# Column sums for a linear-attention denominator: two DMA transposes and a VectorE reduction in place of ten one-column matmuls

## The chip, the cores and the metric

The kernel runs on one core of one Trainium2 chip. Times are device microseconds (us) of that core. A run's time (about 210 us) is some 2 us longer than the span that its profile shows (about 208 us, first to last instruction).

Engines: PE is TensorE's matmul row, PEld its weight loads, DVE is VectorE, ACT is ScalarE, POOL is GpSimd, SP is SyncE, which here issues the DMAs.

## The reference, cut to what matters

```python
xn = _layernorm(x)                                     # 2048 tokens x 640
q, k, v = split(xn @ wqkv)                             # 32 heads of 20
pq, pk = phi(q), phi(k)
kv  = einsum("bhsd,bhse->bhde", pk, v)
z   = einsum("bhsd->bhd", pk)                          # the token sums
num = einsum("bhqd,bhde->bhqe", pq, kv)
den = einsum("bhqd,bhd->bhq", pq, z)[..., None] + 1e-6
out = x + (num / den) @ wo + gelu(xn @ w1 + b1) @ w2 + b2
```

z is one number for each of the 640 columns of phi(k), summed over 2048 tokens. The change concerns only how z gets from "one partial sum per partition" to "one number per column, on the partition where it is needed".

## The kernel before

The kernel plans its instructions by hand. The order in which an engine's instructions are written is the order in which they run in these traces (in the changed kernel's, DVE starts the five ZB products at 105.51 us and the first q unit's operation only at 106.73, though that unit's exp ended at 105.87). It works in stages: layer norm and the gelu branch's first matmuls; the K stage (phi(k) into `PK`); the GT stage (160 matmuls of `PK` and the normalised tokens); the q units (five per chunk of 512 tokens, each five matmuls, an exp on ACT and two DVE operations); the KVT and M steps between the chunks; the denominator (den); and the output matmuls.

During the GT stage DVE adds the sixteen token tiles of `PK` into `zsum` (128 partitions x 640, float) and splits the sum into a bf16 hi and lo part. Then ten matmuls against a column of ones sum each part over the partitions. Column j + 5m of the sums lands on partition m, column j of z.

```python
def z_step():
    b = zbank
    Pl.ins("tensor", [(lambda e, j=j, i=i: e.matmul(bank(b, j, j + 1), zhl[:, i, j:D:DT], onesb[:],
                                                    start=(i == 0), stop=(i == 1)))
                      for j in range(DT) for i in range(2)],
           reads=[r_zhl, r_small], writes=[B_[b]])
    Pl.ins(v, lambda e: e.tensor_copy(z_sb[:], bank(b, 0, DT)), reads=[B_[b]], writes=[r_z])
    for j in range(DT):
        Pl.ins(v, lambda e, j=j: e.tensor_scalar(ZB[:, j, :], bmask[:], z_sb[:, j:j + 1], None, ALU.mult), ...)

def token_sum():
    # ... cut: zsum = sum of the 16 tiles PK[:, t, :], 15 additions
    Pl.ins(v, lambda e: e.tensor_copy(zhl[:, 0, :], zsum), reads=[r_zsum], writes=[r_zhl])
    Pl.ins(v, lambda e: e.tensor_tensor(out=zhl[:, 1, :], in0=zsum, in1=zhl[:, 0, :], op=ALU.subtract), ...)

token_sum()
for f in range(DT):
    b = take(2)
    zbank = (b + 3) % 8
    if f == DT - 1:
        z_step()                      # between GT blocks 4 and 5 in PE's order
    # ... cut: 32 GT matmuls of block f, then ACT copies the two banks out

def phi(src, b, nb, dst, ...):        # one unit: ACT exp, then two operations on DVE
    # exp into one of three buffers ek; min and add in place; max(src, 0) + ek into dst, which frees the bank

q_chunk(0); kvt_step(); q_chunk(1); q_chunk(2); m_step(); q_chunk(3)
# ... cut: den_step() reads ZB; then the output matmuls
```

PSUM's eight banks are handed out in a ring by `take`. The M step takes five pairs of banks, and its fourth pair is the one that the last two q units of chunk 2 used: it must wait until DVE is done with them.

## Time and profile before

| | before |
|---|---|
| time, median of 3 runs | 210.2 us (210.06 to 210.44) |
| span in the profile | 207.9 us |
| PE busy | 203.1 us, 98% |
| DVE busy | 108.1 us, 52% |
| ten ones matmuls on the chain of waits | 0.36 us |
| DVE idle between ZB and the first q unit | 4.56 us |

From the page of the kernel before: busy time by engine, the granted PE clock in forty slices (tenths of full speed), the DMA share in the same slices, and the chain of work that ended last.

```profile
PE 203.1 (98%) x1592; PEld 140.4 (68%) x1598; DVE 108.1 (52%) x226; ACT 74.3 (36%) x141; POOL 21.1 (10%) x59
PEclk9999999999999999999999999999999999999999
DMA  5999779997000000000000000681111111001001
PE 91%; DVE 4%; DMA 3%; issue 1%; ACTq 0%; DVEq 0%
```

PE is the limit: it is busy for 98% of the span, at full clock (1.00 on average over the span), and is 91% of the chain. The DMA engines are idle through the middle of the kernel (share 0.00 from 54 to 124 us).

The chain of waits of the kernel before, pieces in order of time (start, duration, what), around the place that is changed.

```profile
81.80 17.39 PE ps L511 x128
99.18 0.36 PE ps L485 x10
99.54 4.37 PE ps L511 x32
...
122.72 0.70 DVE PQ L463
123.43 0.14 issue
123.56 1.29 PE ps L548 x32
```

The ten ones matmuls (L485) sit in PE's stream between four blocks of GT matmuls and the fifth. The part cut here follows DVE from 115.22 on: its operations for the q units come one unit after another every 1.08 us, which is PE's own pace. The last three lines are the one place downstream where PE follows DVE closely: DVE ends the last q unit of chunk 2 at 123.42, and the M step's fourth group (L548) begins at 123.56.

The timeline of the kernel before (start, duration, engine, line, operation, out<-in; in brackets the idle time before it and who ended it).

```profile
96.63 0.49 DVE L500 CAST Msb<-Msb 128x640 bf16<-128x640 f32 x1
97.16 0.83 DVE L501 TENSOR_TENSOR Msb<-Msb 128x640 bf16<-128x640 f32 x1
99.58 0.17 DVE L489 COPY z_sb<-ps 128x5 f32<-128x5 f32 x1 [1.60 <-PE ps L485]
99.78 1.32 DVE L491 TENSOR_SCALAR ZB<-bmask,z_sb 128x32 bf16<-128x32 bf16 x5
105.03 0.60 ACT L460 ACTIVATE ek<-ps 128x512 bf16<-128x512 f32 x1 [0.38 <-PE ps L523]
105.66 0.29 DVE L461 TENSOR_SCALAR ek<-ek 128x512 bf16<-128x512 bf16 x1 [4.56 <-ACT ek L460]
```

The first two lines make hi and lo. DVE is done with z at 101.1 and is idle until the first q unit: it starts that unit 0.03 us after the exp ends (105.03 + 0.60 to 105.66).

The twelve DMA transposes that the kernel already makes near its start, from the view of their source line.

```profile
L444 SPq DMA_TRANSPOSE xnT<-xn_tm x12: 1200/1277/2067, 15.1 to 31.0; - x12
DMA to landing us min/median/max: 2.6/3.0/4.7
```

Each takes SP's queue about 1.28 us, and its data land 2.6 to 4.7 us after issue starts.

### The profile page before, as it was taken

The page shows a single profiled execution, that of the slowest core. Times are in us where ns is not written, and L with a number is a line of the kernel's source. Part 1 is how long each engine was busy: PE and PEld are TensorE (multiplying, and loading weights), DVE is VectorE, ACT ScalarE, POOL GpSimd, SP SyncE. Part 2 cuts the span into 40 slices and gives each one's busy share as a digit, 9 for nine tenths or more (in the row PEclk, how much of TensorE's full clock was granted, in tenths as well). Part 3 has the DMA queues.
Part 4 walks back from the last instruction along what each step waited for, and adds up shares of the span by engine and source line. Part 5 has one row for each costly group of instructions (what it writes and reads, how often), then busy time and mean ns, then how long its engine had stood idle before and what let it go on. Part 6 is the DMA issues. An engine that isn't in the chain of part 4 may idle for free.

```text
span 207.9 us, 3963 instructions
## 1 busy us (share of the span) xinstructions
PE 203.1 (98%) x1592; PEld 140.4 (68%) x1598; DVE 108.1 (52%) x226; ACT 74.3 (36%) x141; POOL 21.1 (10%) x59
## 2 busy tenths in 40 slices
PE   7899999999999999999999999999999999999995
PEld 2799886444457777777756565577777777777775
DVE  4689960000008888998268865474863422523322
ACT  2689887666676445111153577100000000000000
POOL 3245567000041000000000000000000000000000
PEclk9999999999999999999999999999999999999999
DMA  5999779997000000000000000681111111001001
GB/s 167 343 358 110 119 123 152 372 324 249 3 0 0 0 3 0 0 3 0 0 3 2 0 3 0 202 309 47 71 59 57 63 39 54 32 32 35 32 34 62
DMA packets 22698, 17.98 MB, mean 86 GB/s; under 512 B 9240, under 2 KB 22680, under 8 KB 22680
## 3 DMA queue, kind: packets, MB, share of 16 engines
q1 hardware_dynamic: 22000, 17.24, 29.5%
q10 hardware_dynamic: 680, 0.49, 0.9%
q8 instruction: 12, 0.20, 0.4%
q14 instruction: 6, 0.05, 0.1%
HBM read 12.62 MB, written 2.62 MB: 73 GB/s over the span
## 4 chain that ended last, share of the span: by engine, by line
PE 91%; DVE 4%; DMA 3%; issue 1%; ACTq 0%; DVEq 0%
PE ps L612 33%; PE ps L352 25%; PE ps L511 10%; PE ps L473 10%; PE ps L523 7%; DVE PQ L463 3%; DMA W<-in_B_w_dram 3%; PE ps L648 2%; DVE ek L461 1%; PE ps L532 1%; PE ps L548 1%; PE ps L558 1%; PE ps L382 1%; PE ps L336 0%; ACTq L233 0%
## 5 line engine op out<-in xcount | busy, mean ns | idle before, releaser
L352 PE MATMUL ps<-xnT,W 128*128 128x128 bf16 (+2 forms) x432 | 51.8, 281 | 0.2
L612 PE MATMUL ps<-W,HG 128*128 128x320 bf16 x360 | 51.0, 299 | 0.0
L352 PEld LDWEIGHTS ps<-xnT,W 128*128 128x128 bf16 x435 | 35.5, 98 | 15.6
L612 PEld LDWEIGHTS ps<-W,HG 128*128 128x128 bf16 x360 | 35.1, 98 | 14.2 <-issue 0.4
L356 ACT ACTIVATE HG<-ps,b1c 128x128 bf16<-128x128 f32 (+2 forms) x87 | 40.0, 492 | 12.5 <-PE ps L352 10.3
L461 DVE TENSOR_SCALAR ek<-ek 128x512 bf16<-128x512 bf16 (+1 forms) x36 | 11.1, 308 | 41.7 <-ACT ek L460 40.5
L460 ACT ACTIVATE ek<-ps 128x512 bf16<-128x512 f32 (+1 forms) x36 | 23.2, 644 | 19.8 <-PE ps L523 10.1
L631 DVE TENSOR_TENSOR out_sb<-ps,xnT 128x640 bf16<-128x640 f32 x15 | 12.4, 825 | 33.5 <-PE ps L612 33.3
L612 PE MATMUL ps<-Msb,PQ 128*128 128x320 bf16 x150 | 22.3, 299 | 0.0
L511 PE MATMUL ps<-xPK,xn_tm 128*128 128x320 bf16 x160 | 22.1, 299 | 0.0
L473 PE MATMUL ps<-Wqkv,xnT 128*128 128x320 bf16 x160 | 21.9, 299 | 0.0
L523 PE MATMUL ps<-xnT,Wqkv 128*128 128x512 bf16 x97 | 21.4, 379 | 0.3 <-issue 0.2
L473 PEld LDWEIGHTS ps<-Wqkv,xnT 128*128 128x128 bf16 x160 | 15.6, 98 | 6.3
L511 PEld LDWEIGHTS ps<-xPK,xn_tm 128*128 128x128 bf16 x160 | 15.6, 98 | 6.0
L612 PEld LDWEIGHTS ps<-Msb,PQ 128*128 128x128 bf16 x150 | 14.6, 98 | 5.7
L523 PEld LDWEIGHTS ps<-xnT,Wqkv 128*128 128x128 bf16 x100 | 11.6, 118 | 9.6 <-ACT Msb L553 0.2
L463 DVE SCALAR_TENSOR_TENSOR PQ<-ps,ek 128x512 bf16<-128x512 f32 x20 | 13.8, 692 | 2.1
L308 DVE BATCH_NORM_STATS2 stats<-xPK 128x6 f32<-128x320 bf16 x32 | 13.6, 466 | 2.5 <-DMA xPK<-in_A_x_dram 2.4
L463 DVE SCALAR_TENSOR_TENSOR xPK<-ps,ek 128x640 bf16<-128x640 f32 x16 | 13.2, 825 | 1.7
L498 DVE TENSOR_TENSOR Msb<-Msb,xPK 128x640 f32<-128x640 f32 x14 | 11.6, 826 | 0.5
L515 ACT ACTIVATE W<-ps 128x640 bf16<-128x640 f32 x5 | 3.5, 703 | 18.6 <-PE ps L511 18.6
L318 POOL TENSOR_TENSOR rstd<-aggr,mhalf 128x1 f32<-128x1 f32 x16 | 9.1, 568 | 8.9 <-DVE aggr L316 8.9
(62 smaller groups left out, 90.6 us busy)
## 6 DMA issues: line engine op xcount, KB each, us to landing
xnT<-in_A_x_dram SPq DMA_DIRECT2D x4, 640.0 KB, 6.6
Wqkv<-in_A_wqkv_dram SPq DMA_DIRECT2D x3, 800.0 KB, 6.4
out_dram<-out_sb SPq DMA_DIRECT2D x15, 160.0 KB, 1.8
W<-in_B_w_dram SPq DMA_DIRECT2D x1, 1920.0 KB, 15.6
W<-in_B_w_dram SPq DMA_DIRECT2D x3, 480.0 KB, 6.8
xPK<-in_A_x_dram SPq DMA_DIRECT2D x2, 640.0 KB, 9.4
Wo<-in_A_wo_dram SPq DMA_DIRECT2D x1, 800.0 KB, 10.9
xPK<-in_A_x_dram SPq DMA_DIRECT2D x4, 160.0 KB, 4.2
```

What stands on the lines that cost most here:

```text
L308: Pl.ins(v, lambda e: e.bn_stats(stats[:, s, 6 * h:6 * h + 6], x_in[:, t, h * HW:(h + 1) * HW]), reads=[r_x[t]], writes=[r_stats[s][h]])
L352: Pl.ins("tensor", [(lambda e, k=k: e.matmul(bank(b, 0, w), W1[:, k, jb * P:(jb + 1) * P], xnT[:, k, tok], start=(k == 0), stop=(k == DT - ...
L356: Pl.ins("scalar", lambda e: e.activation(HG[:, jb, tok], bank(b, 0, w), ACT.Gelu_apprx_tanh, bias=b1c[:, jb:jb + 1]), reads=[B_[b], r_b1c ...
L460: Pl.ins("scalar", lambda e: e.activation(e2, src, ACT.Exp), reads=br, writes=[r_ek[s]])
L461: Pl.ins(v, lambda e: e.tensor_scalar(et, et, 1.0, 1e-6, ALU.min, ALU.add), reads=[r_ek[s]], writes=[r_ek[s]])
L463: Pl.ins(v, lambda e: e.scalar_tensor_tensor(out=d2, in0=src, scalar=0.0, in1=e2, op0=ALU.max, op1=ALU.add), reads=br + [r_ek[s]], writes= ...
L473: fns.append(lambda e, k=k, h=h, b=b, t=t: e.matmul(bank(b + h, 0, HW), xnT[:, k, t * P:(t + 1) * P], Wqkv[:, k, D + h * HW:D + (h + 1) * ...
L498: Pl.ins(v, lambda e, t=t: e.tensor_tensor(out=zsum, in0=zsum, in1=PK[:, t, :], op=ALU.add), reads=[r_PK[t], r_zsum], writes=[r_zsum])
L511: Pl.ins("tensor", [(lambda e, t=t, h=h, b=b, f=f: e.matmul(bank(b + h, 0, HW), xn_tm[:, t, f * P:(f + 1) * P], PK[:, t, h * HW:(h + 1) * ...
L523: Pl.ins("tensor", [(lambda e, k=k, j=j, b=b: e.matmul(bank(b), Wqkv[:, k, j:D:DT], xnT[:, k, cc], start=(k == 0), stop=(k == DT - 1))) fo ...
L612: return lambda e: e.matmul(bank(b + h, 0, HW), l, r[:, h * HW:(h + 1) * HW], start=(i == 0), stop=(i == JT + DT - 1))
L631: Pl.ins(v, lambda e: e.tensor_tensor(out=halves(out_sb[:, s, :]), in0=pair(b), in1=halves(x_res[:, t, :]), op=ALU.add), reads=B_[b:b + 2] ...
```

## The change

Its intent: take the ten matmuls off the engine that is the limit, and let engines that are idle there (DMA with its share of 0.00, DVE with its 4.56 us before the first q unit) do the sum over partitions. A DMA transpose turns "640 columns on 128 partitions" into "128 values in a row for each column", and DVE adds along the row. So that column j + 5m lands on partition m, hi and lo are now written in the order (j, m), which makes DVE read `zsum` with a stride of five floats. In DVE's order the wait for the DMA now lies before the q units.

```diff
         def z_step():
-            b = zbank
-            Pl.ins("tensor", [(lambda e, j=j, i=i: e.matmul(bank(b, j, j + 1), zhl[:, i, j:D:DT], onesb[:],
-                                                            start=(i == 0), stop=(i == 1)))
-                              for j in range(DT) for i in range(2)],
-                   reads=[r_zhl, r_small], writes=[B_[b]])
-            Pl.ins(v, lambda e: e.tensor_copy(z_sb[:], bank(b, 0, DT)), reads=[B_[b]], writes=[r_z])
+            zT = out_sb[:].rearrange("p a (j q) -> p a j q", j=DT)
+            for i in range(2):
+                Pl.ins("sync", lambda e, i=i: e.dma_start_transpose(zT[:, i], zhl[:, i, :]),
+                       reads=[r_zhl], writes=[r_out[i]], dma=True)
+            Pl.ins(v, lambda e: e.tensor_reduce(out=z_sb[:], in_=zT.rearrange("p a j q -> p j a q"),
+                                                axis=mybir.AxisListType.XY, op=ALU.add),
+                   reads=r_out, writes=[r_z])
             # ... unchanged: ZB from bmask and z_sb
         def token_sum():
             # ... unchanged: zsum
-            Pl.ins(v, lambda e: e.tensor_copy(zhl[:, 0, :], zsum), reads=[r_zsum], writes=[r_zhl])
-            Pl.ins(v, lambda e: e.tensor_tensor(out=zhl[:, 1, :], in0=zsum, in1=zhl[:, 0, :], op=ALU.subtract),
+            zs = zsum.rearrange("p (m j) -> p j m", j=DT)
+            zp = zhl.rearrange("p a (j m) -> p a j m", j=DT)
+            Pl.ins(v, lambda e: e.tensor_copy(zp[:, 0], zs), reads=[r_zsum], writes=[r_zhl])
+            Pl.ins(v, lambda e: e.tensor_tensor(out=zp[:, 1], in0=zs, in1=zp[:, 0], op=ALU.subtract),
                    reads=[r_zsum, r_zhl], writes=[r_zhl])

         token_sum()
+        z_step()
         for f in range(DT):
             b = take(2)
-            zbank = (b + 3) % 8
-            if f == DT - 1:
-                z_step()
```

## The prediction

> **What bounds the kernel now.** TensorE: busy 203.1 of 207.9 us (page, busy time), full granted clock in every slice; the chain of work that ended last is 91% PE, and PE's waits sum to about 2 us, nearly all at the start. VectorE is at 52%; the DMA engines idle from about 52 to 125 us. So only what changes PE's stream, or makes PE wait, moves the time.
>
> **The stage touched** (timeline, 80 to 130 us). PE runs the 160 GT matmuls (PK and xn) from 81.63. DVE meanwhile adds the token sums (83.74 to 98.0). The ten 128x1 ones matmuls sit before the last GT block, at 99.02, and take 0.36 us of the chain. DVE waits 1.60 us for them, copies z (0.17 us), builds ZB (5 x 0.234 us, done at 101.1), then idles 4.56 us until the first q unit's exp, at 105.66. ZB's reader, the den matmuls, comes only at 133.57.
>
> **What the change does.**
> - Removes ten weight loads and ten matmuls from PE: about -0.4 us, all critical. GT then ends near 103.5, not 103.91, and the first q unit wants DVE near 105.25.
> - Removes the 0.17 us copy from PSUM.
> - The sums are read with a stride of five floats. The cast (0.493 us) should fall to its neighbour's 0.826; the subtract stays at 0.83. hi and lo are ready near 98.35.
> - Adds two DMA transposes on the SP queue. The twelve in this trace take 1.28 us of issue each and land 2.6 us (least; median 3.0) after issue starts. Issues near 98.4 and 99.7; the second lands near 102.4. [...]
> - Adds a reduction of 128x1280 bf16 on DVE. [...] From the instructions here that read PSUM (512 elements 0.69 us, 640 elements 0.825, so 1.06 ns each plus 0.15) I estimate 1.5 us: 102.4 to 104.0. ZB follows until about 105.4.
>
> **How much is critical.** DVE, in order, now waits about 4 us for DMA, in a gap that was idle anyway. It starts the q units about 0.1 to 0.3 us late. In that stage PE makes a unit every 1.08 us and DVE can do one every 1.00 when behind; DVE next holds PE at the banks of the M step (123.41 against 123.55). Counting DVE's work without gaps (15 units and 1.95 us of KVT masks) gives an estimated 0.8 us of slack. So the late start is absorbed and the PE saving stays: about -0.4 us.
>
> **Prediction.** 209.8 us, 80% range 209.3 to 210.7. Faster by over 2%: 0.01; within 2%: 0.97; slower by over 2%: 0.02.
>
> **What would show the steps right.** GT one run of 160 matmuls ending 0.4 us earlier; transposes issued near 98.4 and 99.7, the second landing near 102.4; DVE waiting 3.5 to 4.5 us for DMA; a reduction near 1.5 us; the first q unit's DVE operation at most 0.5 us behind its exp; no new PE wait in the M step.
>
> **What would make it wrong.** Transposes landing over 1 us later, [...] or a reduction over 2.5 us: DVE then starts the q units over 1 us late, the slack is used up, and PE waits for PSUM banks in the q stage or M step, up to 1 us for each further us, as PE has no room to make it up. Slower by 2% (4 us) needs a delay of about 5 us.

210.2 us less the 0.4 us of the ones matmuls is 209.8 us, and the late start of 0.1 to 0.3 us stays below the slack of 0.8 us and adds nothing.

## The result, and the profile after

The changed kernel took 209.86 us (median of 6 runs, 209.46 to 210.53) against 210.2 us for the kernel before in the same rounds. The ratio is 0.9987, with a 95% interval of 0.9968 to 1.0006. Ratios here are the mean time of one kernel's fast runs over that of the other's of the same rounds, so they are not quite the ratio of the medians. In a second set of rounds (e_after_again below) the ratio was 0.9982, interval 0.9970 to 0.9994. So the change is within 2%. The medians put it 0.3 to 0.5 us ahead; the first interval still includes no change, the second does not.

From the page of the changed kernel: busy time by engine, and the chain of work that ended last.

```profile
PE 203.1 (98%) x1582; PEld 140.3 (67%) x1588; DVE 109.7 (53%) x226; ACT 74.3 (36%) x141; POOL 21.1 (10%) x59
PE 94%; DMA 3%; DVE 1%; issue 0%; ACTq 0%; DVEq 0%
```

PE has ten matmuls fewer (1592 to 1582). Its busy total hides the gain, because PE worked longer before the GT stage: the first load of weights on the chain of waits took 5.86 us in place of 5.20, and the GT stage began 0.63 us later. Both lie before the place that was changed.

The chain of waits of the changed kernel in the same place.

```profile
82.42 21.73 PE ps L512 x160
...
122.97 0.70 DVE PQ L463
123.67 0.14 issue
123.81 1.29 PE ps L549 x31
```

The GT stage is one run of 160 matmuls, 21.73 us, where it took 17.39 + 0.36 + 4.37 = 22.12 us before: 0.39 us less. The meeting point at the M step has the same 0.14 us as before, so nothing was given back there.

The timeline of the changed kernel for the same instructions.

```profile
97.26 1.31 DVE L503 CAST Msb<-Msb 128x640 bf16<-128x640 f32 x1
98.61 1.31 DVE L504 TENSOR_TENSOR Msb<-Msb 128x640 bf16<-128x640 f32 x1
99.95 2.53 SPq L486 DMA_TRANSPOSE out_sb<-Msb  x2
103.99 1.49 DVE L488 TENSOR_REDUCE z_sb<-out_sb 128x5 f32<-128x1280 bf16 x1 [4.07 <-DMA out_sb<-Msb]
105.27 0.60 ACT L460 ACTIVATE ek<-ps 128x512 bf16<-128x512 f32 x1 [0.38 <-PE ps L524]
105.51 1.31 DVE L492 TENSOR_SCALAR ZB<-bmask,z_sb 128x32 bf16<-128x32 bf16 x5
106.73 0.29 DVE L461 TENSOR_SCALAR ek<-ek 128x512 bf16<-128x512 bf16 x1
...
122.57 0.29 DVE L461 TENSOR_SCALAR ek<-ek 128x512 bf16<-128x512 bf16 x1
122.97 0.69 DVE L463 SCALAR_TENSOR_TENSOR PQ<-ps,ek 128x512 bf16<-128x512 f32 x1
```

Cast and subtract take 1.31 us each (before 0.49 and 0.83). DVE waits 4.07 us for the transposes. The reduction takes 1.49 us. The first exp ends at 105.87 and DVE takes it up only at 106.73, so DVE is 0.86 us behind (before: 0.03). By the last unit of chunk 2 it has caught up: that exp (not shown) ends at 122.54 and DVE starts at 122.57.

The execution starts 0.6 us later in this trace than in the one before, so from here on I use a stretch without the start: **from the start of the first GT matmul to the start of the last output addition**. Before: 81.63 to 205.65, 124.02 us. After: 82.26 to 205.90, 123.64 us. The change is worth -0.38 us. The end points in the two timelines, first before and then after (of each line only the start counts):

```profile
81.63 4.65 PE L511 MATMUL ps<-xPK,xn_tm 128*128 128x320 bf16 x33
205.65 0.29 DVE L651 TENSOR_TENSOR out_sb<-ps,xnT 128x128 bf16<-128x128 f32 x1 [0.59 <-PE ps L648]
82.26 3.97 PE L512 MATMUL ps<-xPK,xn_tm 128*128 128x320 bf16 x28
205.90 0.29 DVE L652 TENSOR_TENSOR out_sb<-ps,xnT 128x128 bf16<-128x128 f32 x1 [0.59 <-PE ps L649]
```

The expectations below were written with end points that differ by up to 0.2 us from these, so read their differences and not their absolute figures.

### The profile page after: what moved, and what is told of

Same layout as the page of the kernel before. It is cut to its first block, busy times and chain, and to the rows that moved or that the text cites. A ratio compares the mean times of both kernels' runs of the same rounds, so it can differ in the third digit from the quotient of the medians.

```text
span 208.1 us, 3947 instructions
## 1 busy us (share of the span) xinstructions
PE 203.1 (98%) x1582; PEld 140.3 (67%) x1588; DVE 109.7 (53%) x226; ACT 74.3 (36%) x141; POOL 21.1 (10%) x59
## 4 chain that ended last, share of the span: by engine, by line
PE 94%; DMA 3%; DVE 1%; issue 0%; ACTq 0%; DVEq 0%
PE ps L613 33%; PE ps L352 25%; PE ps L512 10%; PE ps L473 10%; PE ps L524 10%; DMA W<-in_B_w_dram 3%; PE ps L649 2%; PE ps L533 1%; DVE PQ L463 1%; PE ps L549 1%; PE ps L559 1%; PE ps L382 0%; PE ps L336 0%; ACTq L233 0%; DVE out_sb L652 0%
```

## The experiments

Theory: PE is the limit, the ten matmuls cost it their full 0.36 to 0.40 us, and DVE's later start on the q units is absorbed, since DVE can do a unit every 1.00 us while PE makes one every 1.08. (In the changed trace DVE starts units at 106.73, 107.73 and 108.73 us while it is behind; in the trace before, exps start at PE's pace at 115.22, 116.30 and 117.38 us.) First rival: the ones matmuls cost PE something else. Second rival: the late start took back a part of the gain, so that a version without it would be faster. Third rival: DVE's lateness never matters, whatever its size.

Each stretch in this table is that of the one profiled execution of its run.

| run | change of the stretch against | stretch, us | DVE behind the first exp, us |
|---|---|---|---|
| before | | 124.02 | 0.03 |
| after | before: -0.38 | 123.64 | 0.86 |
| e_after_again | before: -0.39 | 123.63 | 0.86 |
| e_removed | after: -0.01 | 123.63 | 0.03 |
| e_defer | after: 0.00 | 123.64 | 0.03 |
| e_onetr | after: 0.00 | 123.64 | 0.17 |
| e_contig | after: +0.01 | 123.65 | 0.03 |
| e_late_half | after: +0.82 | 124.46 | 1.71 |
| e_late1 | after: +1.46 | 125.10 | 2.38 |
| e_ones_x4 | before: +1.20 | 125.22 | 0.03 |
| e_ones_x11 | before: +6.93 | 130.95 | 0.03 |

### e_ones_x11: the ones matmuls eleven times over

```diff
-                              for j in range(DT) for i in range(2)],
+                              for r in range(11) for j in range(DT) for i in range(2)],
```

> The kernel before, with the group of ten ones matmuls issued eleven times into the same bank (same z). Theory (TensorE is the limit and every ones matmul is paid in full): ten extra groups at the 0.36 to 0.52 us that one group took give +3.6 to +5.2 us, about 213.8 to 215.4 us. Rival (the matmuls hide in slack of TensorE's queue, so that removing them could save nothing): under +1 us.

Measured: 216.73 us (4 runs) against 210.35 us, ratio 1.0295; result correct. That is above what either theory allowed. The chain of waits of this run says where it went.

```profile
82.12 17.39 PE ps L511 x128
99.50 4.36 PE ps L485 x110
103.86 7.29 PE ps L511 x32
```

The ten extra groups cost 4.36 - 0.36 = 4.00 us, 0.40 us each, as the theory says. But the 32 GT matmuls after them took 7.29 us in place of 4.37. Together these are 6.92 of the 6.93 us. The table by stretch of time (here windows of 2 us; columns: window, its length, busy time and number of PE, PEld, DVE, ACT and POOL instructions, granted PE clock, DMA share, GB/s) shows the reason.

```profile
102.00:104.00 2.00, 2.00 (x49) 1.89 (x48) 0.10 (x1) 0.00 (x0) 0.00 (x0) 0.72 0.03 8
104.00:106.00 2.00, 2.00 (x9) 1.12 (x8) 1.24 (x6) 0.00 (x0) 0.00 (x0) 0.50 0.00 0
106.00:108.00 2.00, 2.00 (x10) 1.08 (x8) 0.00 (x0) 0.00 (x0) 0.00 (x0) 0.50 0.00 0
108.00:110.00 2.00, 2.00 (x10) 1.17 (x9) 0.00 (x0) 0.00 (x0) 0.00 (x0) 0.57 0.00 0
110.00:112.00 2.00, 2.00 (x14) 1.30 (x13) 0.00 (x0) 0.70 (x1) 0.00 (x0) 1.00 0.00 0
```

The granted clock fell to half for about 7 us (two windows at 0.50, and most of the 0.57 and half of the 0.72), although PE is shown busy for the whole of each window. The run's average of 0.984 fits full clock elsewhere: 7 us at half clock take 0.016 from a span of 215.1 us. The 0.72 of the first window puts the fall, as an estimate, at about 102.9 us (0.88 us at 1.00 and 1.12 us at 0.50), so some 3.4 us into the ones matmuls and not after them. The half clock thus began within 4.4 us of one-column matmuls with full busy time in the profile. Why it fell is not shown; no run isolates it. The next run keeps the group short.

### e_ones_x4: four times over

```diff
-                              for j in range(DT) for i in range(2)],
+                              for r in range(4) for j in range(DT) for i in range(2)],
```

> The kernel before with the ones group issued four times, not eleven: short enough, I think, that the granted clock stays at 1.0. Theory (0.36 to 0.40 us of TensorE for each group, and the rest of the eleven-fold run's loss was the clock at 0.50): first GT matmul to the end +1.1 to +1.2 us over before, clock 1.0 throughout. Rival (a group costs about 0.7 us, as the eleven-fold run's total divided by ten says): +2.0 us or more.

Measured: 211.82 us (4 runs) against 210.18 us, ratio 1.0076 (interval 1.0058 to 1.0093); correct; clock 1.000 in the profiled run, whose 40 ones matmuls took 1.56 us. The stretch grew by 1.20 us for three extra groups, 0.40 us each. The timed rounds say more: the medians differ by 1.64 us, and the interval stands for 1.22 to 1.95 us, or 0.41 to 0.65 us for a group. The profile is of the fastest of the four executions (211.21 us, the others 211.55 to 212.22), and the clock of one of the others was 0.998; where their additional time went is not shown. The rival's 2.0 us or more lies just beyond that interval and is not what the trace shows, so it falls. In the traces ten ones matmuls cost PE 0.36 to 0.40 us, and this is what the change takes away.

### e_removed: the ones matmuls taken out, nothing put in

```diff
-            Pl.ins("tensor", [ ... the ten ones matmuls ... ], reads=[r_zhl, r_small], writes=[B_[b]])
-            Pl.ins(v, lambda e: e.tensor_copy(z_sb[:], bank(b, 0, DT)), reads=[B_[b]], writes=[r_z])
+            Pl.ins(v, lambda e: e.tensor_copy(z_sb[:], zsum[:, 0:DT]), reads=[r_zsum], writes=[r_z])
```

> The kernel before with the ones matmuls taken away and nothing put in their place: z is copied from the first five columns of the sums, so the result is wrong on purpose; VectorE is done with ZB near 100 us and never late. Theory (VectorE's late start after the change is wholly absorbed): the stretch from the first GT matmul to the end is 123.7 to 123.8 us as in the changed kernel (before 124.1), time within 0.1 us of the changed kernel. Rival (part of the saving was given back to VectorE's late start): this one is 0.2 us or more faster than the changed kernel over the same stretch.

Measured: 209.67 us (6 runs), ratio 0.9967 (0.9948 to 0.9986) to the kernel before of those rounds; result wrong. The stretch is 123.63 us, the same as the changed kernel's. So the change realises all that removing the ones matmuls can give, and the second rival falls.

### e_defer: the transposes kept, DVE's part moved behind the M step

```diff
         def z_step():
             # ... the two transposes
-            Pl.ins(v, lambda e: e.tensor_reduce(...)); ZB
+            return zT
+        def z_dve(zT):
+            Pl.ins(v, lambda e: e.tensor_reduce(...)); ZB
         ...
         m_step()
+        z_dve(zT_)
         q_chunk(3)
```

> The changed kernel with the reduction and the ZB products moved behind the M step's place in VectorE's order, into its idle 3.4 us there; the transposes stay. Result correct. Theory (lateness is free): same time as the changed kernel within 0.1 us, first GT matmul to end 123.7 to 123.8 us; the first q unit's VectorE operation follows its exp at once. Rival (lateness costs): 0.2 us or more faster over that stretch.

Measured: 209.75 us (6 runs), ratio 0.9968 (0.9949 to 0.9986); correct; stretch 123.64 us. DVE took up the first q unit 0.03 us after its exp, and nothing was gained. Being 0.86 us late was free. This is the safer form of the change, since it leaves DVE no lateness to absorb, but it is no faster.

### e_late1 and e_late_half: how much lateness is free

Each puts one more reduction in front of the real one, of both parts (1.49 us) or of the hi part alone (0.82 us).

```diff
+            Pl.ins(v, lambda e: e.tensor_reduce(out=z_sb[:], in_=...,   # e_late1: again hi and lo; e_late_half: zT[:, 0], axis X
+                                                op=ALU.add), reads=r_out, writes=[r_z])
             Pl.ins(v, lambda e: e.tensor_reduce(out=z_sb[:], in_=zT.rearrange("p a j q -> p j a q"), ...
```

> The changed kernel with its reduction issued twice, so VectorE starts the q units about 1.5 us later still. Theory (the slack in the q stage was about 1.1 us and is used up: in the changed trace VectorE runs the fifteen units and the masks with no gap until the M step): +1.3 to +1.6 us, near 211.3 us, with TensorE held at the M step. Rival (banks and exp buffers give VectorE several us more): under +0.4 us.

> The changed kernel with an extra reduction of the hi half only (640 elements), about 0.85 us more on VectorE. Theory (the changed kernel has used up its slack to the last 0.1 us, and lateness costs one for one from there): +0.7 to +0.85 us over the changed kernel. Rival (there is half a microsecond of slack left): +0.35 us or less.

Measured: e_late1 211.35 us (4 runs, ratio 1.0043 to before), stretch +1.46 us; e_late_half 210.59 us (4 runs, ratio 1.0020), stretch +0.82 us; both correct. From the timeline of e_late_half, the M step and the DVE operation before it:

```profile
123.55 0.69 DVE L463 SCALAR_TENSOR_TENSOR PQ<-ps,ek 128x512 bf16<-128x512 f32 x1
124.39 1.29 PE L552 MATMUL ps<-Wo,W 128*32 128x320 bf16 x32 [0.95 <-DVE PQ L463]
```

And the waits of PE in e_late1 (line that waited, line waited for: us in total, times, longest).

```profile
PE ps L552 <- DVE PQ L463: 1.1, 1, 1.1
PE ps L527 <- DVE PQ L463: 0.4, 1, 0.4
```

PE now waits for DVE at the M step, where the prediction put the meeting point, and in e_late1 in the q stage as well. Take from each lateness what it cost: 1.71 - 0.82 = 0.89 us and 2.38 - 1.46 = 0.92 us. So about 0.9 us of lateness is free, a little less than the 1.1 us in the expectation of e_late1, and the rest is paid almost one for one; the third rival falls. The change uses 0.86 us of it: it just fits.

### e_onetr: one transpose in place of two

```diff
-            for i in range(2):
-                Pl.ins("sync", lambda e, i=i: e.dma_start_transpose(zT[:, i], zhl[:, i, :]), ...)
+            zT10 = out_sb[:].rearrange("p a (j q) -> p (a j) q", j=DT)
+            Pl.ins("sync", lambda e: e.dma_start_transpose(zT10, zhl.rearrange("p a d -> p (a d)")), ...)
```

> The changed kernel with hi and lo sent through one DMA transpose of 128x1280 in place of two of 128x640. Result correct. One issue of 1.2 us fewer would let the reduction start up to 1.3 us earlier, unless the larger transpose takes as much longer to issue. Theory (the late start is absorbed anyway): time and the stretch from the first GT matmul unchanged within 0.1 us of the changed kernel. Rival: 0.2 us or more faster.

Measured: 209.57 us (6 runs), ratio 0.9973 (0.9961 to 0.9985); correct; stretch 123.64 us. From its timeline:

```profile
99.39 1.35 SPq L486 DMA_TRANSPOSE out_sb<-Msb  x1
102.76 1.49 DVE L488 TENSOR_REDUCE z_sb<-out_sb 128x5 f32<-128x1280 bf16 x1 [3.40 <-DMA out_sb<-Msb]
```

One transpose of twice the size issues in 1.35 us and lands 3.3 us after its issue starts, so DVE waits 3.40 us and not 4.07, and is 0.17 us behind and not 0.86. The time does not follow, as the theory says. The 0.14 us between the medians of this run and e_after_again is within the scatter of either.

### e_after_again: the changed kernel beside these

It is the changed kernel without an edit.

> The changed kernel itself, unedited, on the chip of this call, to stand beside the others. First GT matmul to the last output instruction 123.4 to 123.6 us as in its first trace; time about 0.4 us under the kernel before (ratio 0.997 to 0.999).

Measured: 209.71 us (5 runs, 209.66 to 210.02) against 210.18 us, ratio 0.9982 (0.9970 to 0.9994); stretch 123.63 us.

### e_contig: hi and lo without the stride

```diff
-            Pl.ins(v, lambda e: e.tensor_copy(zp[:, 0], zs), ...)
-            Pl.ins(v, lambda e: e.tensor_tensor(out=zp[:, 1], in0=zs, in1=zp[:, 0], op=ALU.subtract), ...)
+            Pl.ins(v, lambda e: e.tensor_copy(zhl[:, 0, :], zsum), ...)
+            Pl.ins(v, lambda e: e.tensor_tensor(out=zhl[:, 1, :], in0=zsum, in1=zhl[:, 0, :], op=ALU.subtract), ...)
```

> The changed kernel with hi and lo written from the sums in their own order, with no stride; the columns of z are then mixed up, so the result is wrong on purpose. If the stride of five floats is what made cast and subtract 1.31 us each: cast back to 0.49, subtract to 0.83, the reduction starts 1.3 us earlier; first GT matmul to the end unchanged (123.4 to 123.6 us). If something else (the write side, the neighbouring DMA) slowed them: still about 1.3 us.

Measured (one look): 209.91 us. Cast and subtract:

```profile
97.31 0.49 DVE L503 CAST Msb<-Msb 128x640 bf16<-128x640 f32 x1
97.84 0.82 DVE L504 TENSOR_TENSOR Msb<-Msb 128x640 bf16<-128x640 f32 x1
```

Only the order of reading and writing differs, and both are back at their old times, so the order is what made them slow: the strided read, since the changed kernel writes hi and lo without gaps. DVE is no longer behind, and the stretch is 123.65 us, unchanged. One warning: the comparison called this result correct, although z's columns are mixed up. The comparison accepts it, so a "correct" does not prove that z's columns are in order. That they are in order in the changed kernel follows from the indices in its code.

### e_strides, e_strides2, e_strides3: what a strided read costs

The kernels add dummy casts behind ZB, each reading floats in some pattern and writing bf16 contiguously. They are late by design, so their total times (218.29, 218.95 and 222.79 us, one look each) say little; all were correct.

```diff
         z_step()
+        for st in (1, 2, 4, 5, 8, 10):      # e_strides: 640 elements, st interleaved columns
+            Pl.ins(v, lambda e, st=st: e.tensor_copy(scr[:].rearrange("p (j m) -> p j m", j=st),
+                                                     scf[:].rearrange("p (m j) -> p j m", j=st)), ...)
+        # also: one with the stride on the write side, two bf16 reads
+        # e_strides2: eight flat reads, 320 elements, strides 1 to 8
+        # e_strides3: eight patterns of 640 elements, listed below
```

> The changed kernel with dummy VectorE casts behind ZB, 640 elements each: float reads with a stride of 1, 2, 4, 5, 8 and 10 elements and contiguous bf16 writes, one with contiguous float reads and bf16 writes of stride 5, two bf16 reads of stride 1 and 5. [...] By way of a dose, VectorE is then some 8 us later and the whole kernel should be 7 to 9 us longer than the changed kernel, TensorE waiting in the q stage.

> The changed kernel with a fill of 2560 floats and eight dummy casts of 320 floats to bf16 behind ZB, contiguous writes, float reads with strides of 1 to 8 elements in one flat access. In the run of strides before, 640 elements took 0.49 us at strides 1 and 2, 0.74 at 4, 8 and 10, and 1.31 at 5. Guess A (an odd stride over 1, one that is no multiple of 8 bytes, is the slow case): strides 3, 5 and 7 about 0.65 to 0.75 us, strides 2, 4, 6 and 8 0.33 to 0.45. Guess B (only 5 with its two-level access is slow, the depth of the access being the cause): all of 3 to 8 alike, near 0.4.

> The changed kernel with a fill of 4096 floats and eight dummy casts of 640 floats (the last: 639) behind ZB, contiguous writes. In order: flat with stride 4; flat with stride 5; five interleaved columns of 128 with stride 5 (the access of the change, 1.31 us before); five blocks one after the other of 128 with stride 5; four of 160 with stride 5; five of 128 with stride 6; five of 128 with stride 7; three of 213 with stride 5. Guess A (the odd stride in a two-level access is slow): the third to fifth, the seventh and the eighth near 1.3, the sixth 0.73. Guess B (only the number of rows, five, an odd one, matters): third, fourth, sixth, seventh and eighth slow, the four of 160 fast. Guess C (a stride of 5 over 640 elements is slow in any form, flat too): the second as slow as the third.

Measured, from the view of the casts' source lines:

| pattern of the float read, contiguous bf16 write | elements | us |
|---|---|---|
| stride 1; two columns of stride 2 | 640 | 0.494; 0.496 |
| 4 columns of stride 4; 8 of 8; 10 of 10 | 640 | 0.742; 0.731; 0.725 |
| **5 columns of stride 5** (the change's) | 640 | **1.305** |
| flat, stride 1; 2; 3; 4 | 320 | 0.327; 0.327; 0.374; 0.441 |
| flat, stride 5; 6; 7; 8 | 320 | 0.446; 0.439; 0.454; 0.446 |
| flat, stride 4; stride 5 | 640 | 0.724; 0.732 |
| 5 columns of stride 5, again | 640 | 1.287 |
| 5 blocks, one after the other, stride 5 | 640 | 0.730 |
| 4 columns, stride 5 | 640 | 0.730 |
| 5 columns of stride 6; of stride 7 | 640 | 1.268; 1.292 |
| 3 columns of stride 5 | 639 | 1.295 |

In e_strides the write with stride 5 took 1.92 us, and the bf16 copy went from 0.326 to 0.862 us with five columns. The lines of e_strides3 for the second, third, fourth and fifth pattern:

```profile
L527 DVE CAST scr<-PQ x1: 732/732/732, 111.6 to 111.6; 128x640 bf16<-128x640 f32 x1
L527 DVE CAST scr<-PQ x1: 1287/1287/1287, 112.4 to 112.4; 128x640 bf16<-128x640 f32 x1
L527 DVE CAST scr<-PQ x1: 730/730/730, 113.7 to 113.7; 128x640 bf16<-128x640 f32 x1
L527 DVE CAST scr<-PQ x1: 730/730/730, 114.4 to 114.4; 128x640 bf16<-128x640 f32 x1
```

Both guesses of the first run fell. One had stride 2 between 0.8 and 1.0 us (measured 0.496) and stride 4 and more near 1.31 us (measured 0.742 at stride 4), the other had every strided read at 0.83 us (measured 0.496 to 1.305). In the second run, the flat odd strides cost no more than the even ones near them, so its guess A fell too, and its guess B held (0.374 to 0.454 us for strides 3 to 8). In the third, guess A (odd stride) fell with the even stride 6 at 1.268 and the four columns at 0.730, guess C fell with the flat 0.732, and guess B was right but for the five separate blocks. What the table shows for a cast is this. For 640 floats, strides 1 and 2 cost 0.49 us. The strides of 4 and more that were tried cost about 0.73 us in one flat run (strides 4 and 5), in five blocks one after the other (stride 5) or in an even number of interleaved columns (strides 4, 5, 8 and 10), and about 1.3 us in an odd number of them (3 or 5 columns, strides 5 to 7). So of the 0.81 us that the change's cast lost, some 0.24 us go with the wide stride and some 0.57 us with the odd number of columns. No run tests why. The subtract was not varied in this way. A cast of four columns and then the fifth alone might be cheaper (four columns of 640 floats in all took 0.730 us); it was not tried, since lateness below 0.9 us is free here.

The dose, by the way: in e_strides DVE was 9.46 us behind and the stretch grew by 8.77 us, against 9.46 - 0.9 = 8.56 us by the rule above. This is not a clean test of the rule: PE waited 6.05 us for DVE at one place, and the granted clock was not full all through (0.984 on average over the run, 1.0 in e_contig).

## Why the prediction was right or wrong, point by point

- **The limit and the size of the gain: right.** The prediction said -0.4 us and 209.8 us; the stretch shows -0.38 and -0.39 us, and the medians are 209.86 and 209.71 us. e_ones_x4 and e_removed show that it is the ones matmuls' own time on PE and all of it.
- **"The cast (0.493 us) should fall to its neighbour's 0.826; the subtract stays at 0.83": wrong.** This is the term that was mis-sized. Both took 1.31 us, 0.97 us more together than predicted. e_contig shows that the strided read is the cause for both. For the cast, e_strides and e_strides3 divide it into the wide stride and the odd number of interleaved columns; for the subtract no run does.
- **The transposes: right in kind and size.** The issue took 1.24 us on average, the data landed 2.6 to 2.7 us after issue starts, and DVE waited 4.07 us. The absolute times were later than predicted, by the 0.97 us above and by the 0.63 us by which this execution's GT stage started later.
- **The reduction: right.** An estimated 1.5 us, measured 1.49 us, and half of the elements took 0.82 us in e_late_half, so 1.05 ns for each further element.
- **"It starts the q units about 0.1 to 0.3 us late": wrong.** It was 0.86 us, mainly because of the cast and the subtract: in e_contig the two together take 1.3 us less, and DVE is not late. The prediction's own test (at most 0.5 us behind) failed.
- **"An estimated 0.8 us of slack", met at the M step's banks: right, and it carried the result.** e_late_half and e_late1 give about 0.9 us, with PE waiting there for DVE beyond it. The mis-sized cast ate nearly the whole slack but no more, so the error did not reach the time. The number was therefore in part lucky. Had there been no slack, the 0.86 us would, as an estimate by the same rule, have been paid: 209.8 + 0.86 is about 210.7 us, the upper end of the predicted range.

## What to carry to other kernels

Here one engine was busy 98% of the time, and the change was worth what it took from that engine's stream (0.36 us of ones matmuls, 0.38 us of the stretch), because what another engine gained in lateness (0.86 us) stayed below the slack (0.9 us) at the next point where the busy engine waits for it. In another kernel, look for both. That slack can be counted from the trace (here 15 units at 1.00 us against 1.08 us, less a step in between) and tested by adding a dummy instruction. A rearranged read was not always free on VectorE here (0.49 us at stride 1, 0.73 us flat at stride 5, 1.3 us in five columns of the same stride), so time the exact access pattern.
